# Gated linear attention followed by a PReLU feed-forward, one core: the PReLU without its linear term, the gates' tiny operations on GpSimd, weights in pairs of blocks, new due times

## The chip, the cores and the metric

The program runs on one core of a Trainium2 chip. The metric is the device time of one execution in microseconds (us). The kernel before took 1188.92 us (median of three runs, 1186.17 to 1190.79); the change is to be judged against that.

## The reference

Inputs are float32 except the two feed-forward weights, which come as float64 and are read as pairs of 32-bit words (`words` in the kernel). B, H, S, D = 4, 8, 768, 48; 3072 tokens, d_model 384, d_ff 2048.

```python
mag = sqrt(a_re**2 + a_im**2); scale = minimum(mag, 0.999) / (mag + 1e-6)
a_re, a_im = a_re * scale, a_im * scale              # the gates
for t in range(S):                                   # a complex state per head
    S_re, S_im = ar * S_re - ai * S_im + k[t] v[t].T, ar * S_im + ai * S_re
    y[t] = q[t] @ S_re
x = y, heads joined: (3072, 384)
h = x @ w_in                                         # (3072, 2048)
out = (maximum(h, 0) + alpha * minimum(h, 0)) @ w_out
```

## The kernel before

Three kinds of work share the engines.

`gates(b, c0, c1)` turns a_re and a_im of one to three chunks of 128 tokens into decays (`decs`) and rotations (`phs`), which go to device memory. There are nine such calls. Most of it runs on VectorE and ScalarE over 384 elements per partition and chunk; a tail of short dependent operations (L309 and L311 on `blk` and `run`, L369 to L382) multiplies block ends together. Then L391 and L393, on the large tiles again, use what the tail made.

`unit(u)`, 24 of them (four batches of six chunks), makes the attention output of one chunk: rotation (L596), per level a decay step on VectorE (L668), a copy on ScalarE (L674), small matmuls (L606) and a masking, then the outputs (`ps_y`, L748 and L756). The result goes through device memory to the tile `xT`.

`mlp(m)`, 14 groups of the tokens: the first two and last two groups are one chunk (128 tokens), the ten between are two (256). A group is 16 blocks f of `ps_h` (three matmuls L799 each, 48 in all), which ScalarE moves to the tile g (L805), and then, chunk by chunk, 16 matmuls into `ps_o` (L815). `ps_h` has two buffers and `ps_o` one. The kernel before uses PReLU(h) = h + (1 - alpha) relu(-h): g holds relu(-h), and the linear part is three further matmuls per chunk (L820) with C = w_in w_out, built at the start in `weights_out` (transposes L495, sums L504 that hold both `ps_h` buffers and `ps_o` until all 16 blocks are done).

The weights come in 32 pieces of 128x384 (float64 words). `to_f32` rebuilds float32 from the words: two ScalarE operations (L446, L449) and six VectorE operations (L451 to L469) per piece, with three buffers `ot` that one piece takes all of.

The order of instructions on every engine is fixed when the program is built. Each kind of work is a generator that yields its next step (engine, estimated time, what it waits for); `Plan.run` picks, among the steps that could start first by its estimates, the one with the lowest due time. All transfers but the first batch's 32 `vsc` (L535, issued by GpSimd) are issued by SyncE (SP), in that order too.

Of the kernel before, what the change touches and what calls it, by code (L numbers as in the profile page):

```python
# [34 lines left out]
class Plan:  # L35
# [17 lines left out]

    def _start(self, step):
        engine, _, after, takes = step[:4]
        t = self.busy.get(engine, 0.0)
        for e in after:
            if isinstance(e[0], str):
                if e not in self.done:
                    return None  # L60
                e = self.done[e]
            t = max(t, e[0] + (self.HOP if e[1] not in (engine, None) else 0.0))
        for r in takes:
            if not r.free:
                return None
            e = min(r.free, key=lambda e: e[0])
            t = max(t, e[0] + (self.HOP if e[1] not in (engine, None) else 0.0))
        return t

    def run(self):  # L70
        while self.tasks:
# [5 lines left out]
            now = min(t for t, _ in ready) + 0.02  # L77
            t, task = min(((t, k) for t, k in ready if t <= now), key=lambda x: x[1][2])
            engine, us, _, takes = task[1][:4]
# [4 lines left out]
            if len(task[1]) > 4:  # L84
                land = self.busy["data"] = max(self.busy.get("data", 0.0), end) + task[1][4] / self.RATE
                event = (land + self.LAND, "data")
# [8 lines left out]
def kernel(  # L95
# [92 lines left out]
    def DVE(n, *after, takes=()):  # L188
        return "DVE", 0.17 + n * 1.05e-3, after, takes

    def ACT(n, *after, takes=()):
        return "ACT", 0.17 + n * 0.85e-3, after, takes

    def PE(us, *after, takes=()):
        return "PE", us, after, takes

    def DMA(kb, *after, takes=()):
        return "SP", 0.5, after, takes, kb

    R = {name: Ring(n) for name, n in dict(  # L200
        KQ=3, PP=1, T=2, V=2, W=2, KT=1, St=2, yT=1, xT=2, g=6, ot=3,
# [8 lines left out]
    nc.vector.memset(bias_tiny, TINY / 4)  # L210
# [6 lines left out]
    def gates(b, c0, c1):  # L217
# [5 lines left out]
        STT = nc.vector.scalar_tensor_tensor  # L223
        ab = work.tile([P, 2, NK * GT], F32, tag="ab", name="ab", bufs=1)[:, :, 0:N]
# [10 lines left out]
        nc.scalar.activation(c, x, AF.Sign, bias=bias_tiny)  # L235
        yield ACT(N, t)
        nc.scalar.activation(d, y, AF.Square, scale=GATE_SCALE)
        t = yield DVE(N, t)
        STT(out=x, in0=c, scalar=TINY, in1=x, op0=ALU.mult, op1=ALU.add)
        t = yield ACT(N, t)  # L240
        nc.scalar.activation(c, x, AF.Square, scale=GATE_SCALE)
# [13 lines left out]
        nc.scalar.activation(e, d, AF.Identity, scale=-MAG_EPS * GATE_SCALE, bias=bias_two)  # L255
# [7 lines left out]
        nc.scalar.activation(c, c, AF.Copy, scale=1.0 / GATE_SCALE)  # L263
# [5 lines left out]
        for p in (x, y):  # L269
            tx = yield DVE(N, t)  # L270
            STT(out=p, in0=p, scalar=-0.5 * GATE_SCALE, in1=d, op0=ALU.mult, op1=ALU.mult)
# [136 lines left out]
    rest_al = consts.tile([P, NF], F32, tag="rest_al")  # L408

    C_sb = consts.tile([P, NK, DM], F32, tag="C_sb")  # L410
# [3 lines left out]
    def pieces():  # L414

        t = yield DMA(8)
        nc.sync.dma_start(rest_al, alpha)
        yield DVE(NF, t)
        nc.vector.tensor_scalar(out=rest_al, in0=rest_al, scalar1=-1.0, scalar2=1.0, op0=ALU.mult, op1=ALU.add)
        if words:  # L420
            wi = w_in.bitcast(U32).rearrange("(c p) (f e two) -> f p c e two", p=P, e=P, two=2)
            wo = w_out.bitcast(U32).rearrange("(f p) (c e two) -> f p c e two", p=P, e=P, two=2)
        else:
            wi = w_in.rearrange("(c p) (f e) -> f p c e", p=P, e=P)
            wo = w_out.rearrange("(f p) (c e) -> f p c e", p=P, e=P)
        for f in range(NF):
            for name, src in (("in", wi), ("out", wo)):
                t = yield DMA(394 if words else 197, takes=(R["g"],))
                raw = raws[name, f] = work.tile(list(src[f].shape), U32 if words else F32, tag="g", name="raw", bufs=6)
# [3 lines left out]
    def to_f32(dst, *key):  # L433

        shape = list(dst.shape)
        ta = yield ACT(DM, ("raw", *key), takes=(R["ot"],) * 3)
        raw = raws.pop(key)
        lo, hi = raw[:, :, :, 0], raw[:, :, :, 1]

        def temp(name):  # L440
            t = work.tile(shape, F32, tag="ot", name=name, bufs=3)
            return t, t.bitcast(U32)


        top, top_u = temp("top")
        nc.scalar.activation(top, hi.bitcast(F32), AF.Abs)  # L446
        tl = yield ACT(DM, ta)
        rest, _ = temp("rest")
        nc.scalar.activation(rest, lo, AF.Copy, scale=2.0 ** -52)  # L449
        t = yield DVE(DM, ta)  # L450
        nc.vector.scalar_tensor_tensor(out=top, in0=top, scalar=F64_SMALL, in1=hi.bitcast(F32),  # L451
                                       op0=ALU.is_ge, op1=ALU.mult)
        R["g"].put(max(t, tl))

        yield DVE(DM // 2)
        num, num_u = temp("num")
        nc.vector.tensor_scalar(out=num_u, in0=top_u, scalar1=3, scalar2=0x3FFFFFFF,
                                op0=ALU.logical_shift_left, op1=ALU.bitwise_and)
        yield DVE(DM)
# [445 lines left out]
```

## Time and profile before

| | |
|---|---|
| timed runs | median 1188.92 us, 1186.17 to 1190.79 |
| profiled execution, its own time | 1183.68 us |
| its span, first to last instruction | 1182.0 us |
| mean granted TensorE clock | 0.891 of full speed |
| busy: TensorE, VectorE, ScalarE, GpSimd | 964.3, 747.4, 489.8, 37.4 us |

The profile is of one execution. Busy times are sums over the span, so a stage has to be looked at by itself. A line number is a line of the kernel before. A TensorE matmul of float32 shows as two instructions, so 48 matmuls are x96. In a group of instructions the columns are line, engine, operation, tiles (out<-in), shapes and count, then busy us and mean ns of one, then the idle time of the engine just before them and what ended it.

### The profile page before, as it was taken

To read this page: it belongs to the slowest core of one execution; us is meant where nothing else is said; L and a number is where in the kernel's file an instruction comes from. 1 tells how busy PE (TensorE), PEld (TensorE's weight loads), DVE (VectorE), ACT (ScalarE), POOL (GpSimd) and SP (SyncE) were. 2 spreads that over 40 slices of the span, in tenths; PEclk is the share of its full clock that TensorE was granted. 3 is DMA by queue.
4 is the path that set the end of the run, shared out by engine and by line. 5 is a ranking of instruction groups with operands and counts; after the bars stand their busy time and mean duration, and the time that the engine had idled before them with its cause. 6 is when DMAs were issued, how large, how long until landed. Compare 5 with 4: busy or idle time off the path is not lost.

```text
span 1182.0 us, 24063 instructions
## 1 busy us (share of the span) xinstructions
PE 964.3 (82%) x10112; PEld 692.0 (59%) x10112; DVE 747.4 (63%) x1347; ACT 489.8 (41%) x984; POOL 37.4 (3%) x59
## 2 busy tenths in 40 slices
PE   0425646687858899998898899989898989999998
PEld 0213423556546658666567577667575677686776
DVE  6768787874977488767665885878387737500000
ACT  3353443734544455455245445454354432330111
POOL 9300000000000000000000000000000000000000
PEclk9865676887957999998999999989998989999999
DMA  9864338527683956583767558662765292210000
GB/s 269 200 130 126 95 112 159 113 87 160 122 187 101 189 150 151 163 165 100 151 160 129 159 115 191 129 175 70 161 134 134 92 188 44 55 28 21 7 14 14
DMA packets 201941, 146.36 MB, mean 124 GB/s; under 512 B 58984, under 2 KB 195664, under 8 KB 201832
## 3 DMA queue, kind: packets, MB, share of 16 engines
q1 hardware_dynamic: 198312, 140.02, 51.3%
q0 software_dynamic: 3520, 4.79, 1.5%
q8 instruction: 80, 1.31, 0.5%
q14 instruction: 29, 0.24, 0.1%
HBM read 116.40 MB, written 47.19 MB: 138 GB/s over the span
## 4 chain that ended last, share of the span: by engine, by line
PE 74%; DVE 10%; ACT 9%; issue 4%; DMA 2%; SPq 1%; DVEq 0%; ACTq 0%
PE ps_o L815 22%; PE ps_h L799 22%; PE ps_lv L606 9%; PE ps_y L748 5%; PE ps_o L820 4%; PE ps_c L504 4%; ACT tmp L283 3%; PE ps_lv L649 3%; PE ps_kv L711 3%; PE ps_y L756 2%; DMA KQ<-in_q_dram 1%; PE ps_kt L701 1%; DVE KQ L668 1%; ACT tmp L398 1%; ACT W L674 1%
## 5 line engine op out<-in xcount | busy, mean ns | idle before, releaser
L799 PE MATMUL ps_h<-xT,w_in_sb 128*128 128x256 f32 (+1 forms) x1344 | 297.2, 373 | 6.5 <-ACT g L805 6.4
L815 PE MATMUL ps_o<-w_out_sb,g 128*128 128x384 f32 x768 | 281.3, 509 | 1.4 <-ACT ot L823 1.4
L668 DVE TENSOR_TENSOR KQ<-KQ,T 96x512 f32<-96x512 f32 x280 | 190.0, 685 | 143.4 <-PE ps_lv L606 107.9
L799 PEld LDWEIGHTS ps_h<-xT,w_in_sb 128*128 128x128 f32 x1344 | 232.2, 201 | 40.3 <-ACT g L805 8.7
L815 PEld LDWEIGHTS ps_o<-w_out_sb,g 128*128 128x128 f32 x768 | 141.8, 195 | 87.1 <-issue 7.6
L805 ACT ACTIVATE g<-ps_h 128x256 f32<-128x256 f32 (+1 forms) x224 | 78.2, 353 | 158.7 <-PE ps_h L799 158.2
L606 PE MATMUL ps_lv<-KQ,W 96*64 96x64 f32 x1920 | 91.8, 244 | 59.6 <-ACT W L674 42.6
L606 PEld LDWEIGHTS ps_lv<-KQ,W 96*64 96x64 f32 x1920 | 74.6, 152 | 103.3 <-ACT W L674 58.8
L504 PE MATMUL ps_c<-w_out_sb,wt 128*128 128x384 f32 x96 | 62.6, 821 | 63.4 <-DVE w_out_sb L469 41.9
L674 ACT COPY W<-KQ 96x512 f32<-96x512 f32 x120 | 74.2, 624 | 25.2 <-DVE KQ L668 16.1
L504 PEld LDWEIGHTS ps_c<-w_out_sb,wt 128*128 128x128 f32 x96 | 28.3, 313 | 86.7 <-ACT top L446 42.2
L769 ACT COPY yT<-ps_y 48x256 f32<-48x256 f32 x96 | 30.9, 366 | 112.7 <-PE ps_y L756 105.0
L283 ACT ACTIVATE tmp<-ab 128x1152 f32<-128x1152 f32 (+2 forms) x27 | 54.9, 2075 | 14.9 <-DVE decays_sb L278 14.9
L823 ACT COPY ot<-ps_o 128x384 f32<-128x384 f32 x24 | 11.5, 477 | 117.3 <-PE ps_o L820 117.3
L748 PE MATMUL ps_y<-A,VL 64*48 64x64 f32 x2688 | 50.9, 225 | 9.6 <-issue 9.6
L626 ACT ACTIVATE A<-ps_lv,rows 128x64 f32<-128x64 f32 x144 | 37.7, 329 | 50.0 <-PE ps_lv L606 49.4
L596 DVE TENSOR_TENSOR KQ<-KQ,PP 96x2048 f32<-96x2048 f32 x24 | 54.7, 2281 | 0.1
L820 PE MATMUL ps_o<-C_sb,xT 128*128 128x384 f32 x144 | 52.8, 496 | 0.0
L748 PEld LDWEIGHTS ps_y<-A,VL 64*48 64x48 f32 x2688 | 45.6, 127 | 10.2 <-issue 10.2
L606 PEld LDWEIGHTS ps_lv<-KQ 96*64 96x64 f32 x768 | 30.6, 155 | 32.0 <-issue 14.7
L495 PE MATMUL ps_wt<-ident,w_in_sb 128*128 128x128 f32 x48 | 11.1, 356 | 45.0 <-DVE w_in_sb L469 44.2
L606 PE MATMUL ps_lv<-KQ 96*64 96x64 f32 x768 | 37.6, 247 | 12.2 <-DVE Aown L629 6.3
(100 smaller groups left out, 1106.1 us busy)
## 6 DMA issues: line engine op xcount, KB each, us to landing
VL<-vsc SPq DMA_DIRECT2D x24, 768.0 KB
T<-decs SPq DMA_DIRECT2D x48, 384.0 KB
vsc<-in_v_dram SPq DMA_DIRECT2D x96, 144.0 KB
KQ<-in_q_dram SPq DMA_DIRECT2D x48, 192.0 KB
KQ<-in_k_dram SPq DMA_DIRECT2D x48, 192.0 KB
PP<-phs SPq DMA_DIRECT2D x48, 192.0 KB
decs<-decays_sb SPq DMA_DIRECT2D x7, 1152.0 KB
phs<-tmp SPq DMA_DIRECT2D x14, 576.0 KB
```

What stands on the lines that cost most here:

```text
L283: nc.scalar.activation(U3[:, o], p.rearrange("p (n l) -> p l n", l=L), AF.Copy, scale=w)
L504: nc.tensor.matmul(sums[c], lhsT=wt[:, c], rhs=w, start=(f == 0), stop=(f == NF - 1))
L596: nc.vector.tensor_tensor(out=KQ, in0=KQ, in1=PP.unsqueeze(1).to_broadcast([D2, 2, H, P]), op=ALU.mult)
L606: nc.tensor.matmul(t[64 * i:64 * i + 64, p], lhsT=weights(4 * i + p), rhs=moving(KQ[:, 0, 4 * i + p]), start=True, stop=True)
L626: nc.scalar.activation(a[:, :, cols], t[:, :, cols], AF.Copy, scale=s)
L668: nc.vector.tensor_tensor(out=x, in0=x, in1=decays(h)[:, i].unsqueeze(3).to_broadcast([D2, H, n, h]), op=ALU.mult)
L674: nc.scalar.copy(W.rearrange("p n t -> p (n t)").rearrange("p (m h) -> p m h", h=h), halves(KQ[:, 1].rearrange("p n t -> p (n t)"), h)[:, ...
L748: nc.tensor.matmul(o, lhsT=vp[64 * i:64 * i + 64, s, e_ * D:(e_ + 1) * D], rhs=a[:, HC * own:HC * (own + 1)], start=(name == "own" and not ...
L799: nc.tensor.matmul(p, lhsT=w_in_sb[:, kk, f * P:(f + 1) * P], rhs=xT[:, kk], start=(kk == 0), stop=(kk == NK - 1))
L805: nc.scalar.activation(gt, p, AF.Relu, scale=-1.0)
L815: nc.tensor.matmul(p, lhsT=G[f][:, cols], rhs=w_out_sb[:, f], start=(f == 0), stop=False)
L820: nc.tensor.matmul(p, lhsT=xT[:, kk, cols], rhs=C_sb[:, kk], start=False, stop=(kk == NK - 1))
```

## The change

- MLP: g is made PReLU(h) itself. ScalarE writes relu((alpha - 1) h), VectorE adds max(alpha, 1) h to it (L818, one operation per block f, which reads `ps_h` and g), and `ps_h` is given back after VectorE. C, its transposes and the three matmuls per chunk are gone. A sign that depends on alpha goes into w_out. The tile g comes as three buffers of six blocks, not six of three.
- Weights: 16 pieces of 128x768. Five VectorE operations per piece instead of six; the last addition is made by two matmuls with the identity (L494, L495) into `ps_w`, and ScalarE (L497) copies the sum back, in two parts per piece. One buffer `wtmp` holds a piece from the first ScalarE operation to the last of its matmuls.
- Gates: the operation that made a_re nonzero (L239) is folded into an ACTIVATE; products of up to 80 elements, the `run` chain and the tail up to L382 go to GpSimd, 342 instructions in all.
- `vsc` rows of the first batch: all on SP, and the first chunk's by themselves, first.
- Plan: estimated hops, ties and due times are new (one table per unit).

```diff
+DUE_0, RATE, UNIT, LEAD, GATES_US, W_FROM, W_TO, G0, G1, G2, LOAD = 119.0, 28.0, 30.0, 13.0, 18.0, 3.0, 130.0, 16.0, 28.0, 59.0, 59.0
+due_of = [DUE_0 + RATE * u for u in range(NU)]
...
+        def small(k, *after):
+            return POOL(k, *after) if k <= SMALL else DVE(k, *after)
+        def on(k):
+            return nc.gpsimd if k <= SMALL else nc.vector
...
-        nc.scalar.activation(c, x, AF.Sign, bias=bias_tiny)
-        STT(out=x, in0=c, scalar=TINY, in1=x, op0=ALU.mult, op1=ALU.add)
+        nc.scalar.activation(x, x, AF.Identity, scale=1.5, bias=bias_tiny)
...
-            yield DVE(4 * k, t)
-            TT(out=m, in0=w[:, 1::-1].unsqueeze(2).to_broadcast([P, 2, 2, k]), in1=pairs_of(u), op=ALU.mult)
-            t = yield DVE(2 * k)
-            TT(out=dst, in0=m[:, 0], in1=m[:, 1], op=ALU.add)
+            yield small(2 * k, t)
+            on(2 * k).tensor_tensor(out=m, in0=w[:, 1::-1].unsqueeze(2).to_broadcast([P, 2, 2, k]), in1=pairs_of(u), op=ALU.mult)
+            t = yield small(2 * k)
+            on(2 * k).tensor_tensor(out=dst, in0=m[:, 0], in1=m[:, 1], op=ALU.add)
...
+        top, rest = tmp[:, 0], tmp[:, 1]
         nc.scalar.activation(top, hi.bitcast(F32), AF.Abs)
         nc.scalar.activation(rest, lo, AF.Copy, scale=2.0 ** -52)
+        nc.vector.tensor_scalar(out=top, in0=top, scalar1=F64_SMALL, scalar2=None, op0=ALU.max)
+        nc.vector.tensor_scalar(out=dst_u, in0=top_u, scalar1=3, scalar2=0x3FFFFFFF,
+                                op0=ALU.logical_shift_left, op1=ALU.bitwise_and)
+        nc.vector.scalar_tensor_tensor(out=dst_u, in0=hi, scalar=0xC0000000, in1=dst_u,
+                                       op0=ALU.bitwise_and, op1=ALU.bitwise_or)
...
+        for i, r in enumerate(parts):
+            nc.tensor.matmul(p, lhsT=ident, rhs=m, start=True, stop=False)
+            nc.tensor.matmul(p, lhsT=ident, rhs=low, start=False, stop=True)
+            nc.scalar.activation(m, p, AF.Copy, scale=scales[i])
+        R["wtmp"].put(e)
...
-            nc.scalar.activation(gt, p, AF.Relu, scale=-1.0)
+            nc.scalar.activation(gt, p, AF.Relu, scale=al_1[:, f:f + 1])
+            r = yield DVE(n, r, first=True)
+            nc.vector.scalar_tensor_tensor(out=gt, in0=p, scalar=al_sm[:, f:f + 1], in1=gt,
+                                           op0=ALU.mult, op1=ALU.add)
             R["h"].put(r)
...
-            for kk in range(NK):
-                e = yield PE(DM * 1.68e-3, ("C", 0))
-                nc.tensor.matmul(p, lhsT=xT[:, kk, cols], rhs=C_sb[:, kk], start=False, stop=(kk == NK - 1))
```

Three places show what moves. First TensorE, where the feed-forward begins. Before, its first `ps_h` matmuls stand behind the last of the 16 sums into `ps_c`, and ahead of them is the start of unit 1 (`ps_lv`):

```order
L495 MATMUL ps_wt<-ident,w_in_sb 128x128 x3
L504 MATMUL ps_c<-w_out_sb,wt 128x384 x3
L649 MATMUL ps_lv<-KQ 64x64 x16
L495 MATMUL ps_wt<-ident,w_in_sb 128x128 x3
L504 MATMUL ps_c<-w_out_sb,wt 128x384 x3
L606 MATMUL ps_lv<-KQ 64x64 x8
L799 MATMUL ps_h<-xT,w_in_sb 128x128 x3
L649 MATMUL ps_lv<-KQ 64x64 x16
```

Now:

```order
L759 MATMUL ps_y<-A_1165,VL 48x2x32 x4
L759 MATMUL ps_y<-A_1213,VL 48x64 x4
L494 MATMUL ps_w<-w_in_sb,ident 128x256
L495 MATMUL ps_w<-wtmp,ident 128x256
L767 MATMUL ps_y<-KQ,St 48x128 x4
L810 MATMUL ps_h<-xT,w_in_sb 128x128 x15
L617 MATMUL ps_lv<-KQ,W 64x64 x8
```

The first `ps_h` now follows the end of unit 1 (`ps_y` with `St`), one unit further on, with 15 of the 16 weight pieces ahead of it.

Second, the tail of a gates call in the middle of the program. Now GpSimd holds it, from the last `blk` products to the tail's end (a part of 34 such rows of one call):

```order
L328 TENSOR_TENSOR tmp<-run,runs 128x12
L330 TENSOR_TENSOR run<-tmp 128x6
L328 TENSOR_TENSOR tmp<-run,runs 128x12
L330 TENSOR_TENSOR run<-tmp 128x6
L387 TENSOR_TENSOR tmp<-blk,runs 128x252
L390 TENSOR_TENSOR off<-tmp 128x7x18
L387 TENSOR_TENSOR tmp<-blk,runs 128x252
L390 TENSOR_TENSOR off<-tmp 128x7x18
L396 TENSOR_TENSOR tmp<-tmp 128x144
L398 TENSOR_SCALAR tmp<-tmp 128x144
L400 TENSOR_TENSOR off<-off,tmp 128x288
```

and VectorE, over the same stretch, holds units' steps and then L409, which waits for that tail:

```order
L679 TENSOR_TENSOR KQ<-KQ,T 96x16x32
L671 TENSOR_TENSOR KQ<-KQ,T 96x512
L640 TENSOR_TENSOR A_4509<-ps_lv,maskown 128x256
L679 TENSOR_TENSOR KQ<-KQ,T 96x8x64 x2
L679 TENSOR_TENSOR KQ<-KQ,T 96x256x2 x2
L640 TENSOR_TENSOR A_4550<-ps_lv,mask_106 128x256
L732 TENSOR_TENSOR St<-St,T 96x384
L679 TENSOR_TENSOR KQ<-KQ,T 96x128x4
L409 TENSOR_TENSOR tmp<-tmp,off 128x2x1152
L735 TENSOR_TENSOR St<-St,ps_kv 96x384
```

Before, all of these stood on VectorE in one queue. From the call's last large product (L330) to L409 VectorE now has 18 instructions of units, and nothing behind L409 can pass it.

Third, the end of TensorE's queue, after the last unit. Before:

```order
L799 MATMUL ps_h<-xT,w_in_sb 128x256 x48
L815 MATMUL ps_o<-w_out_sb,g 128x384 x16
L820 MATMUL ps_o<-C_sb,xT 128x384 x3
L815 MATMUL ps_o<-w_out_sb,g 128x384 x16
L820 MATMUL ps_o<-C_sb,xT 128x384 x3
L799 MATMUL ps_h<-xT,w_in_sb 128x128 x48
L815 MATMUL ps_o<-w_out_sb,g 128x384 x16
L820 MATMUL ps_o<-C_sb,xT 128x384 x3
L799 MATMUL ps_h<-xT,w_in_sb 128x128 x48
L815 MATMUL ps_o<-w_out_sb,g 128x384 x16
L820 MATMUL ps_o<-C_sb,xT 128x384 x3
```

Now:

```order
L767 MATMUL ps_y<-KQ,St 48x128 x4
L829 MATMUL ps_o<-w_out_sb,g 128x384 x16
L810 MATMUL ps_h<-xT,w_in_sb 128x256 x48
L829 MATMUL ps_o<-w_out_sb,g 128x384 x32
L810 MATMUL ps_h<-xT,w_in_sb 128x128 x48
L829 MATMUL ps_o<-w_out_sb,g 128x384 x16
L810 MATMUL ps_h<-xT,w_in_sb 128x128 x48
L829 MATMUL ps_o<-w_out_sb,g 128x384 x16
```

Before, a whole further group of two chunks (43 of its 48 `ps_h`, and 2 x 16 + 2 x 3 of `ps_o`) stood between the last `ps_y` and the first row shown; now 16 matmuls of `ps_o` do.

## Rows read from the trace of the kernel before

**Rows 1.** The page's busy time and share of the span, by engine.

```profile
PE 964.3 (82%) x10112; PEld 692.0 (59%) x10112; DVE 747.4 (63%) x1347; ACT 489.8 (41%) x984; POOL 37.4 (3%) x59
```

**Rows 2.** Three stretches: length, then busy us (x instructions) by engine, clock, DMA.

```profile
0.00:207.50 207.50, 91.00 (x505) 52.65 (x505) 159.56 (x357) 88.20 (x168) 37.41 (x59) 0.72 0.62 156
207.50:420.00 212.50, 161.41 (x2017) 127.43 (x2018) 153.81 (x260) 99.06 (x191) 0.00 (x0) 0.80 0.63 141
420.00:1041.80 621.80, 576.51 (x6991) 412.80 (x6989) 434.03 (x732) 277.63 (x554) 0.00 (x0) 0.96 0.58 132
```

**Rows 3.** TensorE in time where the feed-forward begins: start us, us, what.

```profile
202.20 4.18 PE L504 MATMUL ps_c<-w_out_sb,wt 128*128 128x384 f32 x6 [1.47 <-DVE w_out_sb L469]
207.45 1.08 PE L799 MATMUL ps_h<-xT,w_in_sb 128*128 128x128 f32 x6
```

**Rows 4.** The chain of waits near the end: start us, us, what.

```profile
1041.78 18.95 PE ps_h L799 x86
...
1086.08 20.72 PE ps_h L799 x96
1106.80 10.32 PE ps_o L815 x32
1117.12 1.95 PE ps_o L820 x6
...
1155.23 10.83 PE ps_h L799 x96
```

**Rows 5.** Groups of VectorE instructions, shapes apart.

```profile
L668 DVE TENSOR_TENSOR KQ<-KQ,T 96x512 f32<-96x512 f32 x280 | 190.0, 685 | 143.4 <-PE ps_lv L606 107.9 <-ACT W L674 34.2
L629 DVE TENSOR_TENSOR A<-ps_lv,mask 128x256 f32<-128x256 f32 x72 | 29.8, 414 | 3.2 <-PE ps_y L748 3.2
L460 DVE SCALAR_TENSOR_TENSOR num<-top,num 128x384 uint32<-128x384 uint32 x32 | 17.9, 558 | 1.0
L457 DVE TENSOR_SCALAR num<-top 128x384 uint32<-128x384 uint32 x32 | 12.5, 392 | 1.1
L309 DVE TENSOR_TENSOR tmp<-blk 128x72 f32<-128x72 f32 x49 | 11.2, 229 | 2.0 <-ACT blk L341 0.8
L239 DVE SCALAR_TENSOR_TENSOR ab<-tmp,ab 128x1152 f32<-128x1152 f32 x7 | 9.5, 1355 | 38.4 <-ACT tmp L235 38.4
L239 DVE SCALAR_TENSOR_TENSOR ab<-tmp,ab 128x768 f32<-128x768 f32 x1 | 1.0, 957 | 5.5 <-ACT tmp L235 5.5
```

**Rows 6.** Groups of TensorE instructions.

```profile
L504 PE MATMUL ps_c<-w_out_sb,wt 128*128 128x384 f32 x96 | 62.6, 821 | 63.4 <-DVE w_out_sb L469 41.9 <-ACT wt L498 15.4 <-DVE tmp L309 6.1
```

**Rows 7.** Groups of ScalarE instructions, shapes apart.

```profile
L805 ACT ACTIVATE g<-ps_h 128x256 f32<-128x256 f32 x160 | 60.9, 383 | 128.4 <-PE ps_h L799 128.0
L446 ACT ACTIVATE top<-raw 128x384 f32<-128x384 f32 x32 | 17.3, 542 | 16.7 <-DVE rest L467 16.6
L507 ACT ACTIVATE w_out_sb<-w_out_sb,rest_al 128x384 f32<-128x384 f32 x16 | 9.8, 615 | 56.9 <-PE ps_c L504 56.9
L246 ACT ACTIVATE tmp<-tmp 128x768 f32<-128x768 f32 x1 | 0.8, 843 | 0.1
```

**Rows 8.** ScalarE in time, late in the program.

```profile
1087.47 0.38 ACT L805 ACTIVATE g<-ps_h 128x256 f32<-128x256 f32 x1 [0.88 <-PE ps_h L799]
```

**Rows 9.** Groups of GpSimd instructions.

```profile
L165 POOL TENSOR_SCALAR_AFFINE_SELECT mask<-mask 128x128 f32<-128x128 f32 x4 | 3.1, 764 | 0.1
L172 POOL COPY mask<-mask 64x64 f32<-64x64 f32 x6 | 1.4, 235 | 0.2
```

**Rows 10.** GpSimd, VectorE and SP in time, early in the program.

```profile
16.73 22.66 POOL L535 DMA_DIRECT2D vsc<-in_v_dram  x23 [0.50 <-DMA vsc<-in_v_dram]
27.29 0.36 DVE L464 TENSOR_SCALAR top<-num 128x384 uint32<-128x384 uint32 x1
32.14 1.18 DVE L457 TENSOR_SCALAR num<-top 128x384 uint32<-128x384 uint32 x1
23.99 5.39 SPq L535 DMA_DIRECT2D vsc<-in_v_dram  x6
```

More of the change, by code (lines that the diff above doesn't have):

```diff
@@ L76, in run @@
                     ready.append((t, task))
-            now = min(t for t, _ in ready) + 0.02
-            t, task = min(((t, k) for t, k in ready if t <= now), key=lambda x: x[1][2])
-            engine, us, _, takes = task[1][:4]
+            now = min(t for t, _ in ready) + 0.3
+            t, task = min(((t, k) for t, k in ready if t <= now), key=lambda x: (not x[1][1][5], x[1][2]))
+            engine, us, _, takes, kb, _ = task[1]
             for r in takes:
@@ L457, in to_f32 @@
[L457 to L464 removed]
+        yield DVE(n // 2, ta)
@@ L465, in to_f32 @@
+        yield DVE(n // 2)
+        nc.vector.tensor_scalar(out=top_u, in0=dst_u, scalar1=0xFF800000, scalar2=None,
                                 op0=ALU.bitwise_and)
-        yield DVE(DM, tl)
+        t = yield DVE(n, tl)
         nc.vector.tensor_tensor(out=rest, in0=rest, in1=top, op=ALU.mult)
-        t = yield DVE(DM)
-        nc.vector.tensor_tensor(out=dst, in0=num, in1=rest, op=ALU.add)
-        for _ in range(3):
-            R["ot"].put(t)
-        return t
-    def piece(dst, *key):
-        if words:
-            return (yield from to_f32(dst, *key))
-        t = yield DVE(DM, ("raw", *key))
-        nc.vector.tensor_copy(dst, raws.pop(key))
+        for i, r in enumerate(parts):
+            m, low = dst[:, r], rest[:, r]
+            k = m.free_size()
+            e = yield PE(k * 3.36e-3, t, takes=(R["misc"],))
+            p = ps.tile([P, 512], F32, tag="misc", name="ps_w")[:, 0:k].rearrange("p (r e) -> p r e", r=m.shape[1])
+            nc.tensor.matmul(p, lhsT=ident, rhs=m, start=True, stop=False)
+            nc.tensor.matmul(p, lhsT=ident, rhs=low, start=False, stop=True)
+            t_ = yield ACT(k, e)
+            nc.scalar.activation(m, p, AF.Copy, scale=scales[i])
+            R["misc"].put(t_)
@@ L479, in piece @@
+        R["wtmp"].put(e)
+        return t_
+    def piece(dst, parts, scales, *key):
+        if words:
+            return (yield from to_f32(dst, parts, scales, *key))
+        for r, s in zip(parts, scales):
+            t = yield ACT(dst[:, r].free_size(), ("raw", *key))
+            nc.scalar.activation(dst[:, r], raws[key][:, r], AF.Copy, scale=s)
+        del raws[key]
         R["g"].put(t)
         return t
-    def weights_in():
-        for f in range(NF):
-            done["w_in", f] = yield from piece(w_in_sb[:, :, f * P:(f + 1) * P], "in", f)
@@ new lines, in weights @@
+    def weights(name):
+        for f in range(NF // 2):
+            if name == "in":
+                dst, parts, scales = w_in_sb[:, :, 2 * f * P:2 * (f + 1) * P], (slice(0, 2), slice(2, 3)), (1.0, 1.0)
+            else:
+                dst, parts = w_out_sb[:, 2 * f:2 * (f + 1)], (slice(0, 1), slice(1, 2))
+                scales = al_s[:, 2 * f:2 * f + 1], al_s[:, 2 * f + 1:2 * f + 2]
+            done["w_" + name, 2 * f] = done["w_" + name, 2 * f + 1] = yield from piece(dst, parts, scales, name, f)
```

279 lines of the change are left out of this document (126 added, 153 removed).

## The prediction

> **What bounds the kernel now.** I read the page's busy times, then stretches of time, then the chain of waits near the end, then groups of instructions. Over the whole span TensorE is busy 82% and VectorE 63% [rows 1], but an average hides three stages [rows 2, 3]. Stage A, up to the first matmul of the feed-forward at 207.5 us: VectorE is busy 159.6 us of it (77%), TensorE only 91.0, at a granted clock of 0.72, that is, in part at the lower of its two levels (1.2 and 2.4 GHz). The feed-forward can't begin there: the row before it is the last sum for C, which held its PSUM buffers, and these sums waited 41.9 us for VectorE's weight arithmetic [rows 3, 6]. Stage B, 207.5 to 1041.8, the units with the feed-forward between them: TensorE is busy 161.4 + 576.5 = 737.9 us of 834.3, 88.4%; in the long part of it 92.7% at a clock of 0.96, with VectorE at 70% [rows 2]. Stage C is what is left of the feed-forward, one matmul behind the other at full clock: 48 `ps_h` of 256 columns take 20.72 us, of 128 columns 10.83, 16 `ps_o` 10.32, the three with C 1.95 [rows 4]. So VectorE and the weights' chain set A, TensorE sets B and C.
>
> **What the change takes from TensorE.** Three matmuls with C in each of 24 chunks: 24 x 1.95 = 46.8 us at full clock [rows 4], all of it in B and C, where TensorE is the bound. Building C (62.6 us of L504 [rows 6]) lay in A. What comes there instead is 16 pieces, each 768 columns times two matmuls, that is eight instructions of 384 columns: at 10.32/32 = 0.32 us [rows 4] 2.6 us a piece, at the low clock's 4.18/6 = 0.70 us [rows 3] 5.6.
>
> **VectorE in sum.** Weights, before: 32 pieces of four operations like L460 (0.558) and two like L457 (0.392), some 3.0 us each, 95 us. Now 16 pieces of two operations on 768 elements with two inputs (0.957, as L239) and three with one (an estimate of 0.56: L464's 0.36 for 384 doubled less a fixed part): 3.6 us each, 57 us. L239 goes: nine of up to 1.36, 11 us. 342 operations go to GpSimd, at about 0.2 (L309 on 72 elements 0.229), 68 us. Added: L818, 160 at 0.414 (as L629, from PSUM, 256 columns) and 64 of 128 columns at 0.28 (between L309 and L629): 84 us. So 747 - 95 + 57 - 11 - 68 + 84 = 714 us [rows 1, 5, 10]. ScalarE gains 224 pointer scales at 0.07 (L507's 0.615 against L446's 0.542 [rows 7]), 16 us, and is at 41% [rows 1]: no bound.
>
> **Stage A.** Two chains. The weights: `wtmp` lets one piece through at a time, so a piece costs ScalarE's 0.84 (L246 on 768 [rows 7]), VectorE's 3.6, TensorE's 2.6 to 5.6 (4.3 at the old mean clock of 0.72), some 0.6 for the copy that frees `ps_w` between its two parts, and hops of 0.3: 9.6 us. 15 pieces stand ahead of the first `ps_h`, and the first begins at about 18 us as now: 18 + 15 x 9.6 = 162 us. VectorE: the rows that stand on it up to the first L818 add up, at the durations of their shapes, to 150 us. At the 77% of now [rows 2] that is 194 us, at 85% 176. I take 178 us, between the chain (162) and VectorE (194). More is done by then than before: unit 1 is finished and the third gates call is through, too.
>
> The 32 `vsc` transfers move from GpSimd to SP, 32 issues of up to 0.9 us (six took 5.39 [rows 10]), up to 29 us of SP's queue. Behind them stand the phases of the first gates call; SP has nothing else to do until that call ends on VectorE, and the first chunk's rows are a sixth as large. I cost it at nothing. Without that cover the first unit would be up to 29 us later, and that only counts if the weights' chain is not the later one.
>
> **Stage B.** Before: the feed-forward's 10 double groups and 4 single ones need 10 x (20.72 + 2 x 12.27) + 4 x (10.83 + 12.27) = 545 us, of which 135 stand in stage C, so 410 in B. The other 328 of the 737.9 busy us are 22.8 units, 14.4 each [rows 2, 4]. After: without C the sum is 498 us, stage C holds 94 of it (below), so 404 in B; 22 units at 14.2, 312; together 716 us. At the 92.7% of the long part this takes 773 us, at the 88.4% of all of B 810 [rows 2]. I take 785, nearer the first, since the third gates call, which filled B's weak first quarter (76% busy), now lies in A.
>
> What could lower that share is `ps_h`, whose two buffers are now given back by VectorE. In the trace ScalarE starts 0.10 us after a group of three matmuls has ended (1086.08 + 1.29 against 1087.47) and takes 0.38 [rows 4, 8]; a buffer is wanted again 1.29 us after its end (20.72/16 [rows 4]). With 0.07 more for the pointer, 0.05 for a hop and 0.414 on VectorE [rows 5] it comes after 1.07: 0.2 us to spare, if VectorE is free. The gates' operations of up to 1.36 us stand on that queue, too; this is the first rival.
>
> **Stage C.** Five times 10.32 and 20.72 + 2 x 10.83: 94.0 us, where before it was 135. In single groups a buffer is wanted after 10.83/16 = 0.68 us and comes after some 0.8, so two buffers lose about 0.1 us a block, 3 us in two groups; the double group loses nothing. With 1 us for `ps_o` and 3.7 us from the last matmul to the end of the span: 102 us.
>
> **Sum.** 178 + 785 + 102 = 1065 us of span, against 1182.0. The profiled execution took 1.7 us more than its span and stands 5.2 us under the median of the runs, so I add 7: 1072 us, 9.8% faster. With the low ends (162, 716 at 96% busy = 746, 102, 7) it is 1017, with the high ends (194, 810, 102, 7) 1113.
>
> **GpSimd.** The trace of before has none of its small two-input operations. Its nearest rows are a COPY of 64 columns (0.235) and an AFFINE_SELECT of 128 (0.764) [rows 9], and they bound one from 0.1 (it can't be far under the VectorE rows of the same size) to 0.76. I take 0.2, the COPY's, since the tiles are smaller than its. A gates call of three chunks has a chain of 34 of them with some 3 us of ScalarE between: 34 x 0.2 + 3 = 9.8 us. VectorE has 18 instructions of units between the last large product and L409, some 10 us of busy time by their rows, 14 at its 70%: the chain is just covered. What is bought with it, 68 us of VectorE, counts in A only.
>
> While GpSimd wrote descriptors at 16.73 to 39.39, a one-input operation on VectorE took 1.18 us at 32.14 where its like took 0.36 at 27.29 [rows 10]: two engines that look independent hold each other up. By the Trainium skill (SBUF — State Buffer, "Who interferes with whom") a VectorE operation with two inputs in SBUF also locks out a GpSimd operation that reads SBUF, and the other way round, for the whole instruction. The trace shows the one-input case alone; by that rule the second rival below would happen.
>
> **Rivals.**
> 1. VectorE's queue holds `ps_h`. For: 176 of the 224 blocks f lie in stage B, and with 0.2 us to spare any operation of 0.685 or 1.36 us [rows 5] that is under way makes a block late, half of 0.685, some 0.4 us with the longer ones counted. Against: L818 is put first among what is ready, and units' matmuls stand between the blocks. 176 x 0.4 = 70 us: 1142.
> 2. GpSimd and VectorE take turns. Each of some 34 small operations per gates call holds VectorE for 0.2 us, and each waits for half of an L668: 9 x 34 x 0.2 = 61 us, to which nothing is added once VectorE waits at L409, since GpSimd then runs freely: 1133. Against: VectorE has 25% idle time to give.
> 3. Slower than before: a small GpSimd operation costs like the AFFINE_SELECT, 0.76 us. The chain is then 34 x 0.76 + 3 = 29 us, 15 of them uncovered, with all of VectorE's units parked behind L409 and TensorE behind those: nine calls, 135 us, and some 10 for the first call in A: 1072 + 145 = 1217. It decides from 13 us uncovered per call (0.70 us an operation). Against: the COPY at 0.235.
> 4. The early part gains nothing (the weights' chain stays as slow as before, its first matmuls at the low clock throughout, and A ends at 207): 1101, inside the range.
> 5. TensorE is fuller than it ever was over a long stretch: under 1017.
>
> **Chances.** Forecast with rival 4 (1017 to 1113) 0.64; rival 1 0.13, rival 2 0.11; rival 3 0.05; rival 5 0.07. The range 1015 to 1138 holds the forecast, rival 2 and a part of rival 1. About 0.5% is what a measurement here can tell from no change. Faster by more than that 0.93, within it 0.02, slower 0.05.
>
> **What would show it.** First L810 at 165 to 195 us. In its middle TensorE busy 92 to 93% and VectorE about 75%. No idle time to speak of before L810 with L818 as its releaser: 30 us or more is rival 1. GpSimd's small operations at 0.15 to 0.3, and VectorE's wait at L409 for L400 under 2 us a call: more is rival 2 or 3. L668 still at 0.685 and not longer. Stage C from the last `ps_y` some 100 us. I am wrong if A ends after 210, or the last unit ends after 1010.

## The result and the profile after

The changed kernel took 1106.4 us (median of four runs, 1105.3 to 1109.2) against 1189.9 for the kernel before beside it: a ratio of 0.930 (95% interval 0.927 to 0.934). Forecast: 1072, range 1015 to 1138. The profiled execution took 1105.3 us, its span 1103.6. One stage came out far from its forecast: A ended at 227.5 us, not 178, and so past the 210 at which the prediction called itself wrong; B (until unit 23's rows left, at 1000) took 772 for 785, C 103.6 for 102.

Busy time by engine on the page, which answers to [rows 1] (PE is TensorE, PEld its weight loads, DVE VectorE, ACT ScalarE, POOL GpSimd):

```profile
PE 921.2 (83%) x9952; PEld 647.9 (59%) x9952; DVE 731.6 (66%) x1114; ACT 501.2 (45%) x949; POOL 145.2 (13%) x367
```

Stretches up to the first `ps_h`, to 420 and to the last `ps_y`, with the columns of [rows 2]:

```profile
0.00:227.50 227.50, 118.86 (x841) 62.69 (x841) 160.23 (x232) 102.24 (x166) 51.17 (x133) 0.66 0.63 166
227.50:420.00 192.50, 169.34 (x2112) 127.41 (x2110) 142.37 (x222) 104.66 (x192) 18.38 (x44) 0.93 0.72 169
420.00:998.40 578.40, 534.38 (x6560) 387.97 (x6554) 410.00 (x613) 271.26 (x535) 75.64 (x190) 0.96 0.55 130
```

The long middle is as full as forecast (534.4 of 578.4 us, 92.4%). The first stretch is the odd one: VectorE is busy only 70% of it, and TensorE's granted clock is 0.66 of full speed. TensorE in time where the feed-forward begins [rows 3]:

```profile
226.37 0.59 PE L495 MATMUL ps_w<-wtmp,ident 128*128 128x256 f32 x2
226.89 0.65 PE L767 MATMUL ps_y<-KQ,St 96*48 96x128 f32 x8
227.47 1.60 PE L810 MATMUL ps_h<-xT,w_in_sb 128*128 128x128 f32 x12
```

It begins behind the 15th weight piece and unit 1, as the order said. Its own inputs are no reason to wait so long: the first `w_in` piece was done at 36 us, and the load of unit 0's rows into `xT` was issued at 183. Part of what made the pieces late stands on ScalarE's queue. ScalarE in time, second gates call (L469 opens a piece, L497 closes each of its two parts, L357 and L359 are gates):

```profile
82.24 0.92 ACT L469 ACTIVATE wtmp<-raw 128x768 f32<-128x768 f32 x1
89.00 0.52 ACT L357 COPY blk<-tmp 128x192 f32<-128x192 f32 x1 [5.03 <-DVE tmp L330]
89.33 0.36 ACT L359 ACTIVATE blk<-tmp 128x96 f32<-128x96 f32 x1
96.18 0.21 ACT L357 COPY runs<-blk 128x24 f32<-128x24 f32 x1 [6.49 <-POOL blk L330]
96.30 0.57 ACT L497 ACTIVATE w_out_sb<-ps_w,al_s 128x384 f32<-128x384 f32 x1
99.89 0.58 ACT L497 ACTIVATE w_out_sb<-ps_w,al_s 128x384 f32<-128x384 f32 x1 [0.41 <-PE ps_w L495]
100.37 0.88 ACT L469 ACTIVATE wtmp<-raw 128x768 f32<-128x768 f32 x1
```

L497 starts as soon as L357 has, so it was only parked (held back by the fixed order, not by its own inputs) behind it, while L357 waited 6.49 us for GpSimd. This piece took 18.1 us; the shortest took 9.2. From 17.2 to 227.3 us fifteen pieces went through, 14.0 each.

The chain near the end [rows 4]: the double group's `ps_h` costs 0.4 us more than before. In a single group the chain now goes from every second block's matmuls through ScalarE and VectorE to the next but one, which needs the same buffer, 1.78 us for two blocks, so that the group's `ps_h` takes 13.8 us (1051.83 to 1065.62) and not 10.83.

```profile
1009.18 21.12 PE ps_h L810 x96
...
1055.11 0.95 PE ps_h L810 x6
1056.09 0.38 ACT g L816
1056.49 0.36 DVE g L818
1056.89 0.95 PE ps_h L810 x6
...
1064.01 1.61 PE ps_h L810 x12
1065.62 10.32 PE ps_o L829 x32
```

Groups [rows 5, 7, 9], VectorE, then GpSimd:

```profile
L679 DVE TENSOR_TENSOR KQ<-KQ,T 96x512 f32<-96x512 f32 x280 | 191.6, 693 | 81.7 <-PE ps_lv L617 51.3 <-ACT W L685 29.6
L818 DVE SCALAR_TENSOR_TENSOR g<-ps_h,al_sm,g 128x256 f32<-128x256 f32 x160 | 76.2, 481 | 120.9 <-ACT g L816 119.5
L818 DVE SCALAR_TENSOR_TENSOR g<-ps_h,al_sm,g 128x128 f32<-128x128 f32 x64 | 22.2, 349 | 59.6 <-ACT g L816 59.5
L477 DVE TENSOR_SCALAR w_in_sb<-wtmp 128x768 uint32<-128x768 uint32 x8 | 7.6, 953 | 0.3
L477 DVE TENSOR_SCALAR w_out_sb<-wtmp 128x768 uint32<-128x768 uint32 x8 | 4.5, 559 | 0.2
...
L328 POOL TENSOR_TENSOR tmp<-blk 128x72 f32<-128x72 f32 x49 | 21.4, 437 | 114.7 <-ACT blk L359 41.6 <-ACT A L637 34.5 <-DVE KQ L679 19.2
L330 POOL TENSOR_TENSOR run<-tmp 128x6 f32<-128x6 f32 x48 | 13.0, 271 | 3.8
```

Units' rows leave through L780 (L769 before). Those of unit 3, after and then before:

```profile
295.50 1.27 ACT L780 COPY yT<-ps_y 48x256 f32<-48x256 f32 x4
```

```profile
345.57 1.02 ACT L769 COPY yT<-ps_y 48x256 f32<-48x256 f32 x3 [8.24 <-PE ps_y L756]
```

From unit 3's to unit 21's rows (to the end of the last copy) it is 661 us after (296.8 to 957.9) and 659 before (347.9 to 1006.8), 110 per three units in both; the feed-forward finished 17 chunks in that time after, 14 before. So by place, not by cause, the span's 78.4 us came as 51 us by unit 3 (43 of them still there at unit 23) and 35 behind the last unit; the units themselves run no faster.

### The profile page after: what moved, and what is told of

Same layout as the page of the kernel before. It is cut to its first block, busy times and chain, and to the rows that moved or that the text cites. A ratio compares the mean times of both kernels' runs of the same rounds, so it can differ in the third digit from the quotient of the medians.

```text
span 1103.6 us, 23784 instructions
## 1 busy us (share of the span) xinstructions
PE 921.2 (83%) x9952; PEld 647.9 (59%) x9952; DVE 731.6 (66%) x1114; ACT 501.2 (45%) x949; POOL 145.2 (13%) x367
## 4 chain that ended last, share of the span: by engine, by line
PE 60%; DVE 14%; ACT 8%; POOL 7%; issue 5%; SPq 3%; DMA 2%; DVEq 0%; ACTq 0%; POOLq 0%
PE ps_o L829 21%; PE ps_h L810 18%; PE ps_lv L617 6%; PE ps_y L759 5%; POOL tmp L328 3%; PE ps_kv L722 2%; POOL blk L330 2%; DVE tmp L328 2%; PE ps_y L767 2%; SPq L544 2%; DVE KQ L679 2%; PE ps_lv L660 2%; DVE g L818 2%; ACT tmp L301 2%; ACT g L816 2%
## 5 line engine op out<-in xcount | busy, mean ns | idle before, releaser
L810 PE MATMUL ps_h<-xT,w_in_sb 128*128 128x256 f32 (+1 forms) x1344 | 302.4, 373 | 18.7 <-issue 10.7
L810 PEld LDWEIGHTS ps_h<-xT,w_in_sb 128*128 128x128 f32 x1344 | 227.5, 197 | 63.4 <-DVE g L818 21.3
L818 DVE SCALAR_TENSOR_TENSOR g<-ps_h,al_sm,g 128x256 f32<-128x256 f32 (+1 forms) x224 | 98.4, 443 | 180.5 <-ACT g L816 179.0
L816 ACT ACTIVATE g<-ps_h,al 128x256 f32<-128x256 f32 (+1 forms) x224 | 98.9, 443 | 140.1 <-PE ps_h L810 139.2
L617 PEld LDWEIGHTS ps_lv<-KQ,W 96*64 96x64 f32 x1920 | 70.5, 144 | 68.4 <-ACT W L685 32.6
L617 PE MATMUL ps_lv<-KQ,W 96*64 96x64 f32 x1920 | 86.4, 234 | 19.9 <-ACT W L685 15.0
L308 POOL TENSOR_TENSOR decays_sb<-decays_sb 128x72 f32<-128x72 f32 (+8 forms) x37 | 16.8, 454 | 586.5 <-DVE decays_sb L308 584.3
L685 ACT COPY W<-KQ 96x512 f32<-96x512 f32 x120 | 74.7, 622 | 36.2 <-DVE KQ L679 35.6
L494 PE MATMUL ps_w<-w_in_sb,ident 128*128 128x512 f32 (+1 forms) x32 | 23.6, 836 | 55.9 <-POOL blk L330 24.7
L780 ACT COPY yT<-ps_y 48x256 f32<-48x256 f32 x96 | 31.1, 368 | 66.6 <-PE ps_y L767 63.7
L495 PE MATMUL ps_w<-wtmp,ident 128*128 128x384 f32 (+2 forms) x64 | 43.8, 781 | 8.1 <-DVE wtmp L488 7.9
L328 DVE TENSOR_TENSOR tmp<-tmp 128x576 f32<-128x576 f32 (+2 forms) x63 | 43.2, 686 | 6.3 <-ACT tmp L301 5.6
```

What stands on the lines that cost most here:

```text
L328: on(2 * k).tensor_tensor(out=m, in0=w[:, 1::-1].unsqueeze(2).to_broadcast([P, 2, 2, k]), in1=pairs_of(u), op=ALU.mult)
L495: nc.tensor.matmul(p, lhsT=ident, rhs=low, start=False, stop=True)
L617: nc.tensor.matmul(t[64 * i:64 * i + 64, p], lhsT=weights(4 * i + p), rhs=moving(KQ[:, 0, 4 * i + p]), start=True, stop=True)
L685: nc.scalar.copy(W.rearrange("p n t -> p (n t)").rearrange("p (m h) -> p m h", h=h), halves(KQ[:, 1].rearrange("p n t -> p (n t)"), h)[:, ...
L810: nc.tensor.matmul(p, lhsT=w_in_sb[:, kk, f * P:(f + 1) * P], rhs=xT[:, kk], start=(kk == 0), stop=(kk == NK - 1))
L816: nc.scalar.activation(gt, p, AF.Relu, scale=al_1[:, f:f + 1])
```

## The experiments

**Where stage A went: the gates' small operations (two runs).** Theory 1 was the parking shown above; theory 2 the weights' chain by itself. In both runs

```diff
-            return POOL(k, *after) if k <= SMALL else DVE(k, *after)
+            return tiny(k, *after) if k <= SMALL else DVE(k, *after)
```

(and likewise for the `run` chain and the tail), with `tiny` on VectorE where b == 0, or always.

> The tiny gate operations of the first batch only (three calls, all in stage A) are put back on VectorE, the later six calls stay on GpSimd. In the changed kernel the 15 weight pieces ahead of the first ps_h took 17.2 to 227.3 us, 14.0 us each, while the shortest took 9.2. Theory 1 (the gates' chain of alternate GpSimd and ScalarE steps makes ScalarE wait in its own order, 5 to 6 us at a time at L357, and the weight pieces stand behind it): stage A ends at 195 to 212, the time is 1075 to 1092. Theory 2 (the weights' chain is slow by itself: one wtmp, TensorE at a low granted clock, other work on ScalarE between): stage A stays at 225 or ends later, since VectorE gets some 25 us more work there; the time is 1104 to 1118.

> All tiny gate operations back on VectorE, all else as in the changed kernel. Theory 1: stage A ends at 195 to 212 as in the run with the first batch alone; in stage B VectorE gets some 228 operations of 0.2 to 0.25 us, about 50 us, at 70% busy, of which 0 to 15 show: 1080 to 1105. Theory 2: stage A unchanged or later, so 1104 to 1130. Third view (the move to GpSimd is what lets stage B run as it does): stage B longer by 20 to 45 us, 1100 to 1135 with a shorter stage A.

Measured: first `ps_h` at 199.6 and 202.7, as theory 1 said, and yet 1106.5 us (ratio 0.934, 0.929 to 0.938) and 1102.5 (0.930, 0.925 to 0.936): no gain. With the small operations off GpSimd stage A was 25 to 28 us shorter, and its end was not worth them: in the first run B took 801 us (199.6 to 1000) for 772. Two windows of the changed kernel, then of the first run:

```profile
270.00:300.00 30.00, 28.26 (x435) 23.51 (x434) 26.89 (x48) 20.32 (x38) 2.69 (x4) 1.00 0.60 136
300.00:330.00 30.00, 21.73 (x169) 15.94 (x167) 21.29 (x38) 8.79 (x26) 14.32 (x36) 0.72 0.41 118
```

```profile
270.00:300.00 30.00, 25.03 (x390) 17.99 (x388) 28.12 (x37) 17.59 (x24) 1.01 (x3) 1.00 0.57 129
300.00:330.00 30.00, 12.41 (x144) 10.34 (x143) 22.11 (x38) 9.76 (x29) 13.03 (x36) 0.50 0.42 114
```

TensorE is busy 12.4 us there instead of 21.7 and drops to its lower level. It has done two chunks of feed-forward by 288 us (before that edit by 309), and the next group needs units 2 and 3; unit 3's rows left at 301, not earlier than the 297 before that edit. TensorE from 304 us, in that run:

```profile
304.38 1.12 PE L619 MATMUL ps_lv<-KQ,W 96*64 96x64 f32 x16 [1.22 <-DVE A L642]
307.74 1.12 PE L619 MATMUL ps_lv<-KQ,W 96*64 96x64 f32 x16 [2.23 <-DVE A L642]
```

The same steps in the changed kernel have the feed-forward between them:

```profile
302.00 4.14 PE L829 MATMUL ps_o<-w_out_sb,g 128*128 128x384 f32 x12
306.06 0.69 PE L617 MATMUL ps_lv<-KQ,W 96*64 96x64 f32 x16
```

The second run also says what the move to GpSimd is worth: VectorE is 790.2 us busy instead of 731.6, unit 3's rows leave 8 us later (304.5), and the time is the same.

```profile
303.23 1.28 ACT L782 COPY yT<-ps_y 48x256 f32<-48x256 f32 x4
```

**The planner's price.** `0.12 + n * 1.9e-3` became `0.3 + n * 2.2e-3`.

> Only the planner's price of a GpSimd operation is changed, from 0.12 + 1.9e-3 n to 0.30 + 2.2e-3 n us, near what the trace shows (0.20 to 0.23 for 6 to 12 elements, 0.26 to 0.44 for 36 to 72, 0.68 for 252). Theory 1: the plan now knows that the gates' chain is long and puts weight pieces ahead of ScalarE's waiting steps: stage A ends at 205 to 220, the time is 1082 to 1098. Theory 2: no change beyond 5 us, 1100 to 1111.

Measured: first `ps_h` at 226.4, 1102.0 us (0.930, 0.925 to 0.935). Theory 1's numbers were missed and theory 2's met; the price matters little.

**The linear term alone (two runs).** In the kernel before: C, its transposes and sums dropped, the scales by alpha and L818 added; then the same with the two rules of order:

```diff
-            now = min(t for t, _ in ready) + 0.02
-            t, task = min(((t, k) for t, k in ready if t <= now), key=lambda x: x[1][2])
+            now = min(t for t, _ in ready) + 0.3
+            t, task = min(((t, k) for t, k in ready if t <= now), key=lambda x: (not x[1][1][5:] or not x[1][1][5], x[1][2]))
...
+            r = yield DVE(n, r, first=True)
+            nc.vector.scalar_tensor_tensor(out=gt, in0=p, scalar=al_sm[:, f:f + 1], in1=gt,
+                                           op0=ALU.mult, op1=ALU.add)
```

> The kernel before with the linear term alone changed: no C, Relu with alpha's scale and one VectorE operation per block f; weights, gates and due times as before. If the three C matmuls are worth what TensorE spent on them: 46.8 us less in stages B and C, and stage A ends 10 to 20 us earlier because the sums for C, which waited 41.9 us for weights, are gone: 1120 to 1140. Rival: the VectorE operation between ps_h and its buffer's return, which this older plan does not put first, gives much of that back: 1150 to 1175, with idle time of TensorE before ps_h that VectorE ends of 30 us or more.

> The kernel before with the linear term alone changed, as in the run of 1378 us, and with the changed planner's two rules for order: a step marked first (the Relu and the VectorE operation of a block f) goes ahead of all others that are ready within 0.3 us. If that marking is what lets the feed-forward run between the units: the units end at 1030 to 1045 as before, with a tail of 102 instead of 135, and stage A is 0 to 20 us shorter without the sums for C: 1130 to 1160. Rival (the older plan's due times or VectorE's fuller queue hold the feed-forward back whatever its order): above 1250.

Measured: 1378.3 us without (1.162, 1.156 to 1.168), 1155.6 with (0.972, 0.965 to 0.979). Both expectations of the first missed, by far; the second came as its first theory had it. The page of the first, TensorE and VectorE in 40 slices of 34 us:

```profile
PE   0023144566736776645746765789999999999998
...
DVE  6898998688697797698798687775111221112211
```

Its units were through at 956, 87 us earlier than before, but only four of 24 chunks of feed-forward were: the other 20 followed by themselves at 20.7 us each. A block needs ScalarE and then VectorE before its `ps_h` buffer is free, and, with the latest due time of all, each of these steps was last among what was ready. Put first, the feed-forward runs between the units again; the units end at 1045, as before, and what follows takes 102 us instead of 139. So the linear term alone is worth 35.6 us, all of it in stage C, and the two rules of order 223; the two were not tried apart. In both runs the first `ps_h` began at 136 us, 71 earlier than in the kernel before, with no sums to hold its buffers; in the second the units ended no sooner for it.

**C's time put back.** Three more matmuls a chunk in the changed kernel:

```diff
+            for kk in range(NK):
+                e = yield PE(DM * 1.68e-3)
+                nc.tensor.matmul(p, lhsT=xT[:, kk, cols], rhs=w_out_sb[:, kk], start=False, stop=(kk == NK - 1))
```

> The changed kernel with three more matmuls of 384 columns per chunk, in the place and of the shape of those with C (they use the first blocks of w_out, so the values are not the reference's). The runs so far: stage A ended 28 and 25 us earlier (199.6 and 202.7 against 227.5) and the time stayed at 1106.5 and 1102.5, with the units at the same places from the seventh on. Theory 3 (in stage B the chain of units and gates calls sets the pace, 111 us for three units before and after, and TensorE has idle time there): only what stands after the last unit counts, some five chunks, 5 x 1.95 = 10 us: 1112 to 1124, last unit's ps_y within 6 us of 998. Theory of the prediction (TensorE's sum sets stage B): all 24 count, 46.8 us: 1145 to 1158.

Measured: 1163.7 us (0.977, 0.970 to 0.985), 57 more; theory 3 fell, and the prediction's view of TensorE held, with 10 us beyond it. Most of these 10 are in the matmuls themselves, which were busy 55.2 us and not 46.8. The units' rows ended 10 us later (1010), the rest is tail: seven chunks stood behind the last unit instead of five. The feed-forward takes what the units leave; more work there is work at the end.

```profile
L834 PE MATMUL ps_o<-w_out_sb,xT 128*128 128x384 f32 x144 | 55.2, 505 | 0.0
```

Unit 3's rows were as early here as in the changed kernel (294.4 at their end):

```profile
294.07 0.37 ACT L780 COPY yT<-ps_y 48x256 f32<-48x256 f32 x1
```

So with C's matmuls back and all else of the change kept, 27 of the 83 us are left.

**Due times (three runs).** LEAD 13 to 30; DUE_0 119 to 99; and DUE_0 99 with the first batch's small operations on VectorE and the corrected price.

> The changed kernel with LEAD 30 in place of 13: a gates call is due 30 us of the plan's time ahead of the first unit that needs it. Theory 3, if the units wait for the phases (a call's phases left at 571 to 574 and the unit that needed them began at 587): stage B is 10 to 35 us shorter, 1070 to 1098. If it is the sum of VectorE's and TensorE's work in the three units that sets 111 us, and not the wait for the phases: within 6 us of 1106. If earlier gates calls only push the units behind them on VectorE: 1112 to 1130.

> The changed kernel with DUE_0 99 in place of 119: every unit (and the gates calls from the third on) is due 20 us of the plan's time earlier against the weights, whose window stays. Seen so far: the end of stage A moved by 28 us and the time did not, because the feed-forward then ran out of units' rows (TensorE busy 3.1 to 6.7 of 10 us between 290 and 330). Theory 4 (in the first 350 us the units' arrival sets the time, and VectorE's order between weights and units can bring it forward): unit 3's rows leave before 285 instead of 296, the time is 1085 to 1100. Rival (VectorE's whole work up to there sets both, so that one gains what the other loses): 1102 to 1112.

> Three edits together, as a version that may beat both: the first batch's tiny gate operations on VectorE, the planner's GpSimd price corrected, DUE_0 99. Each of the first two moved stage A or the middle a little (1106.5 and 1102.0). Theory 4: units and feed-forward both come earlier, 1080 to 1096. Rival: what sets the time is the sum of work, 1098 to 1110.

Measured: 1118.4 (0.941, 0.935 to 0.947), 1107.3 (0.932, 0.927 to 0.937) and 1104.0 us (0.932, 0.926 to 0.937; its four runs lie between 1094.7 and 1112.1). With earlier gates the units ended at 978, 22 us earlier, and the time grew by 12: the feed-forward fell behind and what followed the last unit took 137 us instead of 104. That is the time of the third expectation, not its mechanism: the units were not pushed back. Earlier due units left unit 3 where it was (300 and 298 for 297), so both rivals held. These due times gain nothing here.

**Work taken out, or moved (three runs).** The weights without their low words (L471, L485, L488, L495 left out); the low words kept in the raw tile, so that two of a smaller `wtmp` fit; L488 on GpSimd, with the first batch's small operations on VectorE in exchange and the corrected price.

```diff
-        tmp = work.tile([P, 2] + list(dst.shape[1:]), F32, tag="wtmp", name="wtmp", bufs=1)
-        top, rest = tmp[:, 0], tmp[:, 1]
+        top = work.tile(list(dst.shape), F32, tag="wtmp", name="wtmp", bufs=2)
+        rest = lo.bitcast(F32)
...
-        nc.vector.tensor_tensor(out=rest, in0=rest, in1=top, op=ALU.mult)
+        nc.gpsimd.tensor_tensor(out=rest, in0=rest, in1=top, op=ALU.mult)
```

> The changed kernel, with the weights taken from their high words alone: the low word's two VectorE operations (0.95 + 0.96 us), its ScalarE operation (0.89) and its matmuls are left out in all 16 pieces, some 31 us of VectorE, 14 of ScalarE and half of TensorE's part in a piece. If VectorE's and the pieces' work in stage A sets the units' arrival: unit 3's rows leave at 265 to 280, 1070 to 1090. If the feed-forward waits for units whose pace has another cause: stage A ends 20 us or more earlier and the time stays at 1100 to 1110.

> The changed kernel with the low words' products kept in the raw tile, so that wtmp is half as large and there are two of it: the next weight piece may begin on ScalarE and VectorE while the matmuls and copies of the one before are still to come. Same operations, same engines. Leaving out the low words brought the time to 1083.6, but took away VectorE's work, TensorE's and a part of the chain at once. If the chain of pieces (14.0 us each, 9.2 at the least) is what counted: stage A ends at 185 to 210 and the time is 1080 to 1096. If VectorE's sum of work in the first 300 us counted: stage A may end earlier, unit 3's rows still leave at 290 to 300, and the time is 1100 to 1112.

> The first batch's tiny gate operations on VectorE, the planner's GpSimd price corrected, and in exchange the low words' product of every piece (0.96 us on VectorE, 15 us in all) on GpSimd, at an estimated 1.5 to 2 us each from the 0.68 of 252 elements and the 1.1 of 288. If VectorE's sum of work counts: unit 3's rows leave before 290 and the time is 1085 to 1098. If the chain of pieces counts, which gets 0.6 to 1.1 us longer per piece: 1104 to 1120.

Measured: 1083.6 us (0.912, 0.909 to 0.916), 1103.7 (0.926, 0.924 to 0.929) and 1120.2 (0.940, 0.937 to 0.944). Unit 3's rows, in that order:

```profile
284.29 1.30 ACT L771 COPY yT<-ps_y 48x256 f32<-48x256 f32 x4 [0.92 <-PE ps_y L758]
```

```profile
296.70 1.30 ACT L780 COPY yT<-ps_y 48x256 f32<-48x256 f32 x4 [0.90 <-PE ps_y L767]
```

```profile
303.63 1.29 ACT L782 COPY yT<-ps_y 48x256 f32<-48x256 f32 x4 [0.88 <-PE ps_y L769]
```

Two pieces under way came out as their second expectation had it; without the low words the time was in the first one's range and unit 3 some 5 us behind it; the low words on GpSimd lie at the upper end of their second.

In these three the time goes with unit 3's rows (285.6, 298.0 and 304.9 at their end), but that is no rule: with all small operations on VectorE they left at 304.5, too, and the time was 1102.5, not 1120.2. It doesn't go with the weights' chain either. With two pieces under way the last `w_in` part was done at 204 instead of 227, but the first `ps_h`, behind unit 1 in TensorE's order, began at 223.8, and the time stayed. Without the low words the last matmuls of a piece ended at 179.5, and the first `ps_h` still stood behind unit 1:

```profile
177.88 1.65 PE L486 MATMUL ps_w<-w_out_sb,ident 128*128 128x384 f32 x2 [0.67 <-ACT w_out_sb L488]
...
214.22 0.64 PE L758 MATMUL ps_y<-KQ,St 96*48 96x128 f32 x8
...
215.26 1.60 PE L801 MATMUL ps_h<-xT,w_in_sb 128*128 128x128 f32 x12
```

The run without low words loses VectorE, ScalarE and TensorE work at once; how its 23 us divide was not tried apart. None of the versions that compute all of it is clearly faster than the changed kernel: 1102.0 to 1104.0 us lie within what the intervals allow.

## Why the prediction held, and where it failed

- **Sum and range.** 1106.4 is inside 1015 to 1138, 34 us above the forecast: A's 49 too many, less B's 13 too few. That C's matmuls cost TensorE time which shows in the end holds: 57 us when they are put back, for 46.8 of matmuls by the forecast and 55.2 by that run's trace.
- **Stage A, the step that failed.** "18 + 15 x 9.6 = 162" had a piece's own cost right (the shortest took 9.2) and left out what stands between its steps on ScalarE's and VectorE's queues: 14.0 measured, 17.2 + 15 x 14.0 = 227. Putting the small operations back on VectorE took away 25 to 28 of the 49 us by which A was late; the others are not divided. VectorE's own sum was nearer (160 us for 150), but its share was 70% and not 77 to 85%, since it waited for L469 (32.5 us in ten waits). And unit 1, behind which the order puts the first `ps_h`, had no chain of its own in the sum: without the low words it was unit 1 that ended A, at 215.3.
- **Adding the stages, the deeper fault.** The sum took A's end as worth its time. Two runs moved it by 25 to 28 us for nothing. In the first of them the feed-forward had used up units 0 and 1 by 288 us, and unit 3, the second that the next group needs, came at 301; that the rows of units 2 and 3 are what has to come early fits this, but is not shown for the whole time.
- **Where the gain comes from.** Two thirds of it, 57 of 83 us, hang on C's matmuls: with them back, unit 3 is as early as without. So the 51 us by which unit 3 was early, which the text had only as "more is done by then", do not bring their time by themselves. Leaving C out of the kernel before gave 35.6 us, and all the rest of the change without that 27; the other 20 or so came only with both. Which part of the rest earned its share (the weights in pairs, the new due times and hops, the `vsc` rows) no run separates; the GpSimd move it was not.
- **Stage B.** TensorE's busy sum was right (705 us for 716) and its share in the long middle too (92.4%). That the length was right, 772 for 785, is partly luck: it is what was left between an A that came 49 us late and the end, and where A ended at 199.6 B took 801. The units' pace is the same as before; the TensorE time that C gave free went into the feed-forward's lead, and showed at the end.
- **Stage C.** 103.6 for 102. Double groups lose 0.4 us for nothing forecast, single groups 3.0 each for 1.5: the return by VectorE was the right mechanism, at twice the size.
- **Sizes.** L818 0.481 and 0.349 for 0.414 and 0.28; a piece's one-input operations on `w_in` views 0.953 for 0.56; a small GpSimd operation 0.27 to 0.44 for 0.2, so that the third call's chain took 19 us (189.8 to 208.9) for 9.8.
- **Rivals.** 1 did not come, though its sign was near: before L810 TensorE's matmuls wait 7.3 us for L818 and its weight loads 21.3, 28.6 by the profile's sum (30 was the mark), 8.8 of them in stage C. That marking L818 first is what prevents it is suggested by the runs of 1378 and 1156 us in the older plan, not tried in the changed kernel. 2 and 3 did not come by their price: VectorE waits 7.7 us for L402 at L409, in two calls, 6.6 of them in one call in stage A (2 was the mark), though the two engines do take turns (below). 4's time, 1101, came closest, for another reason: its A ended at 207, and the units were not early.

## What to carry to other kernels

Don't add stage lengths where a low-priority stream fills the gaps of another: ask which rows it eats and when they come, and count work at the end by what is left over when the other stream ends. A chain over two in-order queues parks everything queued behind its waits; but before repairing that, shorten it once and see whether the end moves. When a step that frees a scarce buffer is moved to a busy engine, its place in that engine's order can be worth far more than its duration. And put a term that was taken out back into the finished kernel, alone: the time that it costs there is the part of the gain that hangs on it.

## What the runs showed of the hardware

GpSimd's and VectorE's two-input operations take turns. In the changed kernel the same GpSimd operation took 0.23 us at 197.18 and 0.95 and 1.01 beside two such VectorE operations, and ended just behind each. Beside a one-input VectorE operation of 0.56 us a smaller one took 0.49, where it took 0.20 by itself at 197.49, so a one-input operation can hold it too:

```profile
197.18 0.23 POOL L328 TENSOR_TENSOR tmp<-run,runs 128x12 f32<-128x12 f32 x1 [0.38 <-ACT runs L359]
197.49 0.20 POOL L330 TENSOR_TENSOR run<-tmp 128x6 f32<-128x6 f32 x1
198.87 0.49 POOL L330 TENSOR_TENSOR run<-tmp 128x6 f32<-128x6 f32 x1
199.43 0.95 POOL L328 TENSOR_TENSOR tmp<-run,runs 128x12 f32<-128x12 f32 x1
201.02 1.01 POOL L328 TENSOR_TENSOR tmp<-run,runs 128x12 f32<-128x12 f32 x1
```

```profile
198.74 0.56 DVE L477 TENSOR_SCALAR w_out_sb<-wtmp 128x768 uint32<-128x768 uint32 x1
199.33 0.96 DVE L480 SCALAR_TENSOR_TENSOR w_out_sb<-raw,w_out_sb 128x768 uint32<-128x768 uint32 x1
200.99 0.96 DVE L488 TENSOR_TENSOR wtmp<-wtmp 128x768 f32<-128x768 f32 x1
```

The other way round in the run with the low words on GpSimd, where VectorE's L609 takes 2.28 us alone:

```profile
137.88 2.77 POOL L490 TENSOR_TENSOR wtmp<-wtmp 128x768 f32<-128x768 f32 x1 [10.01 <-DVE wtmp L487]
138.89 3.91 DVE L609 TENSOR_TENSOR KQ<-KQ,PP 96x2048 f32<-96x2048 f32 x1
```

There 15.3 us of VectorE's work were taken away and its busy time rose from 749.5 (the first batch's run) to 756.4. This is the rule weighed ahead of the result, of the Trainium skill (SBUF — State Buffer, "Who interferes with whom"): whichever began first holds the other for its whole length. The trace agrees for both orders: 0.95 and 1.01 us for 0.23 where VectorE began first, 3.91 for 2.28 where GpSimd did.
